# Fetching all channel weights at once on SyncE's queue, and converting them behind the attention's last cast

## The chip, the cores and the metric

The kernel runs on one core of one Trainium2 chip. The time is the device time of one execution in microseconds, lower is better. A core has five engines with a queue each: TensorE (PE in the profile; PEld is its weight load), VectorE (DVE), ScalarE (ACT), GpSimd (POOL) and SyncE (SP), which here only issues DMAs. Each engine runs its own queue in order; the engines meet through semaphores.

## What is computed

Three layers follow one another on four batches of 576 tokens with 512 channels: windowed attention, a layer of four attention experts of which each token uses two, and a mixing layer. The change lies at the passage from the second to the third, whose weights arrive in float64:

```python
# third layer
theta = x @ w_theta
zr, zi = x * cos(theta), x * sin(theta)
y = einsum('ts,bsd->btd', w_tok_r, zr) + einsum('ts,bsd->btd', w_tok_i, zi)
u = x + y
return u + maximum(u @ w_ch, 0)          # w_ch: the channel weights, 512 x 512
```

## The kernel before

All products run in a split form: an operand is a high part (rounded to the matmul's format) and a low part (the rest), and `mm3` (L97) adds three products, high by high (L98), high by low (L99) and low by high (L100). `split` (L90) makes the two parts, the high one mostly by an ACT cast (L92), the low one by a subtraction on DVE or POOL (L95).

The order of each engine's queue is fixed when the kernel is built: a planner goes through the traced operations by priority (the order in the program, where `merge` interleaves several generators by their costs) and puts each operation down when its operands and its place in memory are free by the planner's own clock. `tc.issue_after(x)` adds the rule that what is traced inside stands behind x on x's engine. At run time each engine follows its fixed order and waits where data are late.

The stages around the change, in order of time. `attn(3, 1)` is the last of the experts' attention, five steps t = 0 to 4, each ending with the cast of its output `oh` (L92, by way of L492). Beside it run `load_tok` (the token weights `w64k`, nine loads of 576 KB, converted in `load64`), `fuse` (products of `w_o` and `w_theta`, which read `wtl` for the last time), then `wo(3)` (output products, stored to DRAM from `xs3a` and `xs3b`) and `theta(0, 0)`. In `theta(b, dh)` five angles come one after the other: products into a bank `bs`, the ACT activation L640, the DVE subtraction L641 (which frees the bank), the ACT sine and absolute value L643 to L645, the DVE product L648 with a transposed `xk` (L636, bank `tb`), an ACT cast and a POOL subtraction into `z`. The fifth angle's products are the small `zf` (L662). Two places hold `ang`, for two angles each. Then `mix(0, 0)` multiplies `z` with the token weights, beside `theta(0, 1)`, `mix(0, 1)` follows beside `theta(1, 0)`, and `channel(0)` multiplies with the channel weights. `halves` makes further token weights in `x2a`, `x2b` and `wtl`.

`load_ch` (L835) brings the channel weights in eight half rows of 128 x 256 float64 (256 KB each) and hands each to `load64` (L105): one DMA from ACT's queue (L108; `late`, set in the attention, makes it stand behind an early exponential), two ACT multiplications (L122, L123), a DVE shift (L124) and a DVE merge of the sign (L130), a POOL addition (L132), an ACT cast (L137) and a DVE subtraction (L138). The staging places are two: for even k one place `bmsx` that holds the raw data and the working data, for odd k the places `VD0` (raw) and `VD1` (working). A load can thus be issued only when the conversion two before it has ended. Three conversions are traced beside `mix(0, 0)`, five beside `mix(0, 1)`.

Of the kernel before, what the change touches and what calls it, by code (L numbers as in the profile page):

```python
# [3 lines left out]

# [9 lines left out]
U32 = mybir.dt.uint32  # L14
I32 = mybir.dt.int32
U64 = mybir.dt.uint64
# [5 lines left out]
P = 128  # L22
# [11 lines left out]
NC = DM // P  # L34
# [6 lines left out]
def f32(ap):  # L41
    return ap.bitcast(F32)


def merge(*parts):

    live = [[0.0, float(total), gen] for total, gen in parts]
    while live:
        p = min(live, key=lambda x: x[0] / x[1])
        cost = next(p[2], None)  # L50
        if cost is None:
            live.remove(p)
        else:
            p[0] += cost
# [3 lines left out]
def kernel(ctx, tc, qT, kT, vw, consts, w_in, w_o, w_th, w_tk, w_ch, outT):  # L58
    nc = tc.nc

    cp = ctx.enter_context(tc.tile_pool(name="cp", bufs=1, side="left"))
# [16 lines left out]
    wtl = cp.tile([P, NC, DM], F32R, tag="wtl", name="wtl")  # L78
# [7 lines left out]
    def pool_mul(out, in_, by):  # L86
        nc.gpsimd.tensor_scalar(out=out, in0=in_, scalar1=by, scalar2=1.0,  # L87
                                op0=ALU.mult, op1=ALU.mult)

    def split(dst_h, dst_l, src, eng_h, eng_l):  # L90
        if eng_h is nc.scalar:
            nc.scalar.copy(out=dst_h, in_=src)  # L92
        else:
            eng_h.tensor_copy(out=dst_h, in_=src)
        return eng_l.tensor_sub(out=dst_l, in0=src, in1=f32(dst_h))  # L95
# [7 lines left out]


    def load64(kind, st, tu, dst_h, dst_l, src, scale=1.0):  # L105
        if late[0]:
            with tc.issue_after(late[0].ins):
                nc.scalar.dma_start(st, src)  # L108
        else:
            with tc.issue_after(last_load[0].ins):  # L110
                nc.sync.dma_start(st, src)
        v = st.bitcast(U32).rearrange("p (n two) -> p n two", two=2)
        lo, hi = v[:, :, 0], v[:, :, 1]
        n = KN["DP"][kind]
        step = st.shape[1] // n
        full = lo, hi, tu[:, 0], tu[:, 1], dst_h, dst_l
        for k in range(n):
            lo, hi, t, u, dst_h, dst_l = (x[:, step * k : step * k + step] for x in full)
            if KN["DM"][kind]:
                nc.gpsimd.tensor_scalar(out=f32(t), in0=f32(hi), scalar1=2.0**-112, scalar2=1.0, op0=ALU.mult, op1=ALU.mult)  # L120
            else:
                nc.scalar.mul(out=f32(t), in_=f32(hi), mul=2.0**-112)  # L122
            nc.scalar.mul(out=u, in_=lo, mul=2.0**-29)  # L123
            shift = lambda: nc.vector.tensor_scalar(out=t, in0=t, scalar1=3, scalar2=None, op0=ALU.logical_shift_left)  # L124
            if kind == 1 and gated[0]:
                with tc.issue_after(gated[0].ins):
                    shift()
            else:
                shift()
            nc.vector.scalar_tensor_tensor(out=t, in0=hi, scalar=0x80000000, in1=t,  # L130
                                           op0=ALU.bitwise_and, op1=ALU.bitwise_or)
            nc.gpsimd.tensor_add(out=t.bitcast(I32), in0=t.bitcast(I32), in1=u.bitcast(I32))  # L132
            if scale == 1.0:
                if KN["DH"][kind]:
                    nc.vector.tensor_copy(out=dst_h, in_=f32(t))
                else:
                    nc.scalar.copy(out=dst_h, in_=f32(t))  # L137
                (nc.vector if KN["DL"][kind] else nc.gpsimd).tensor_sub(out=dst_l, in0=f32(t), in1=f32(dst_h))  # L138
            else:
                nc.scalar.activation(out=dst_h, in_=f32(t), func=AF.Copy, scale=scale)  # L140
                nc.vector.scalar_tensor_tensor(out=dst_l, in0=f32(t), scalar=scale, in1=f32(dst_h),
                                               op0=ALU.mult, op1=ALU.subtract)
# [20 lines left out]
    bp = tc.alloc_tile_pool(name="bp", bufs=1, side="right")  # L163
# [54 lines left out]
    last_v = [None]  # L218
    late = [None]
    gated = [None]  # L220
    X = {b: xbuf[b % 2] for b in range(B)}

    ahead = {}
# [188 lines left out]
    def attn(b, ep):  # L412
# [7 lines left out]
        for t in range(5):  # L420
# [11 lines left out]
            for i in range(2):  # L432
                e = 2 * ep + i
                n = f"{b}{e}{t}"
# [55 lines left out]
                          pT[:, j, i, :m], start=(j == t - 1), stop=False)  # L490
            nc.tensor.matmul(o[:, :m], VD[ep][:, t].rearrange("p h d -> p (h d)"), pT[:, t, 0, :m], start=(t == 0), stop=True)
            split(oh[:, q0 : q0 + m], ol[:, q0 : q0 + m], o[:, :m], nc.scalar, nc.vector)  # L492
            if t == 4:
                for k, x in enumerate((oh, ol)):
                    nc.sync.dma_start(od[b][:, 2 * ep + k], f32(x))
            yield 0.4 * (t + 1)

    def wo(b):
        for n0, n1 in ((0, 320), (320, 576)):
            for m in range(NC):  # L500
                g = bank([P, n1 - n0], ("gggg", ("as", "ta", "g", "g"), ("as", "g", "ta", "g"))[KN["WB"][b]][m], f"x2{b}{m}{n0}")
                for c in range(2):
                    oh, ol = O[b, c]
                    mm3(g, woh[c][:, m * P : (m + 1) * P], wol[c][:, m * P : (m + 1) * P],
                        oh[:, n0:n1], ol[:, n0:n1], c == 0, c == 1)
                nc.scalar.copy(out=x2T[b][:, m, n0:n1] if b < 2 else xs[b][m // 2][:, m % 2, n0:n1], in_=g)
                if b > 1 and n1 == S and m % 2:
                    nc.sync.dma_start(xd[b][:, m - 1 : m + 1], xs[b][m // 2])
                yield 0.75


    HW = DM // 2
# [44 lines left out]
    def load_pair(b):  # L557
        xt = kp.tile([P, NC, P], F32, tag="xt", name=f"xt{b}")
        xo = kp.tile([P, 4, P], F32R, tag="xo", name=f"xo{b}")
        for k in range(2):  # L560
            sl = slice(64 * k, 64 * k + 64)
            if b == 0:
                pool_mul(xt[:, :, sl], x2T[b + k][:, :, W4:], 1.0)
            else:
                nc.sync.dma_start(xt[:, :, sl], xd[b + k][:, :, W4:])
            nc.sync.dma_start(f32(xo[:, :, sl]), od[b + k][:, :, W4:])
        XT[0] = xt, xo
# [262 lines left out]
    def load_tok(cs):  # L830
        for c in cs:
            load64(1, *staging(f"k{c}", S), wkh[c], wkl[c], w_tk[c * P : (c + 1) * P])
            yield 1.0

    def load_ch():  # L835
        for k in range(2 * NC):
            c, sl = k // 2, slice(HW * (k % 2), HW * (k % 2) + HW)
            if k % 2:
                st = bp.tile([P, HW], U64, tag="VD0", name=f"w64c{k}")
                tu = bp.tile([P, 2, HW], U32, tag="VD1", name=f"wtuc{k}")  # L840
            else:
                su = rp.tile([P, 2, HW], U64, tag="bmsx", name=f"w64c{k}")
                st, tu = su[:, 0], su[:, 1].bitcast(U32).rearrange("p (two n) -> p two n", two=2)
            load64(2, st, tu, wch[c][:, sl], wcl[c][:, sl], w_ch[c * P : (c + 1) * P, sl])
            yield 0.5

    def delay(cost, gen):
# [65 lines left out]
                  "x2a": (rp, 1), "x2b": (rp, 1), "x3a": (kp, 1), "x3b": (kp, 1)})  # L913
    load_o(3)
    load_pair(0)
    merge((KN["WO"][3], wo(3)), (KN["CW"][0], theta(0, 0)))
    wc = [bp.tile([P, DM], F32R, tag=f"wo{x}{c}", name=f"wc{x}{c}") for c in range(2) for x in "hl"]
    wd = [bp.tile([P, 2, DM], F32R, tag="vg", bufs=2, name=f"wd{c}") for c in range(2)]
# [79 lines left out]
```

## Time and profile before

| | us |
|---|---|
| median of 3 runs | 512.54 |
| lowest and highest run | 511.04, 513.37 |
| the profiled execution | 512.65 |
| its span in the trace | 510.9 |

In the profile a line such as L108 is a line of the kernel's file. Views in order of time give start, duration, engine, line, operation, output and input by the program's names, and in brackets the idle time of the engine just before with what ended it. ACTq and SPq are the queues' own work, such as issuing a DMA. Raw channel data are `w64c` (working data of even k too, since both share a place), the working data of odd k are `wtuc`; `wch` and `wd` are high parts, `wcl` and `wd` low parts. The granted TensorE clock is 1.00 in all stretches read below.

### The profile page before, as it was taken

The page shows a single profiled execution, that of the slowest core. Times are in us where ns is not written, and L with a number is a line of the kernel's source. Part 1 is how long each engine was busy: PE and PEld are TensorE (multiplying, and loading weights), DVE is VectorE, ACT ScalarE, POOL GpSimd, SP SyncE. Part 2 cuts the span into 40 slices and gives each one's busy share as a digit, 9 for nine tenths or more (in the row PEclk, how much of TensorE's full clock was granted, in tenths as well). Part 3 has the DMA queues.
Part 4 walks back from the last instruction along what each step waited for, and adds up shares of the span by engine and source line. Part 5 has one row for each costly group of instructions (what it writes and reads, how often), then busy time and mean ns, then how long its engine had stood idle before and what let it go on. Part 6 is the DMA issues. An engine that isn't in the chain of part 4 may idle for free.

```text
span 510.9 us, 12108 instructions
## 1 busy us (share of the span) xinstructions
PE 482.4 (94%) x4128; PEld 446.9 (87%) x4128; DVE 368.0 (72%) x1274; ACT 346.9 (68%) x1072; POOL 328.1 (64%) x455
## 2 busy tenths in 40 slices
PE   7898899999999999999999999799999989999997
PEld 5687888889898999988878779699999889899997
DVE  4766887866977768745888775878569948884832
ACT  6947787866787868857786796786276716762720
POOL 6758799864685863335683556578649926792770
PEclk9999999999999999999999999999999999999999
DMA  7665233431335341111245735431353044202002
GB/s 249 191 199 164 82 122 112 128 112 63 121 90 185 111 162 53 33 48 48 68 137 182 262 108 188 135 86 42 97 172 80 6 140 129 63 23 94 1 0 94
DMA packets 45470, 55.92 MB, mean 109 GB/s; under 512 B 6496, under 2 KB 34144, under 8 KB 45408
## 3 DMA queue, kind: packets, MB, share of 16 engines
q1 hardware_dynamic: 43392, 50.36, 31.8%
q10 hardware_dynamic: 2016, 4.79, 2.8%
q8 instruction: 33, 0.54, 0.5%
q14 instruction: 29, 0.24, 0.2%
HBM read 43.34 MB, written 11.80 MB: 108 GB/s over the span
## 4 chain that ended last, share of the span: by engine, by line
PE 50%; DVE 20%; ACT 12%; POOL 7%; DMA 5%; issue 5%; SPq 0%; POOLq 0%; DVEq 0%; ACTq 0%
PE as L272 3%; PE bpt L473 3%; PE qk L98 2%; ACT ams L285 2%; PE apt L297 2%; PE qk L99 2%; PE qk L100 2%; PE bs L441 2%; DMA wst<-in_dram 2%; PE c L98 2%; DMA w64c<-in_dram 2%; PE ao L153 2%; PE c L100 2%; DVE ang L648 2%; PE c L99 2%
## 5 line engine op out<-in xcount | busy, mean ns | idle before, releaser
L285 ACT ACTIVATE ams<-ams,anm 128x128 f32<-128x128 f32 x144 | 56.6, 396 | 6.1 <-DVE anm L277 4.8
L292 POOL TENSOR_TENSOR ams<-ams,arc 128x384 f32<-128x384 f32 x48 | 40.4, 844 | 25.5 <-DVE arc L291 11.5
L87 POOL TENSOR_SCALAR QD<-qt 64x192 f32<-64x192 f32 x72 | 39.7, 551 | 19.2 <-PE as L272 12.5
L450 ACT ACTIVATE bms<-bms,bnm 64x64 f32<-64x64 f32 (+4 forms) x80 | 44.8, 561 | 9.2 <-DVE bnm L445 8.7
L272 PE MATMUL as<-kt,QD 128*128 128x128 f32 x288 | 42.1, 283 | 4.0 <-ACT x0h L92 1.3
L277 DVE CUSTOM_DVE_ANT_0 ams<-as,cst 128x128 f32<-128x128 f32 x144 | 34.9, 284 | 11.8 <-PE apt L297 8.0
L272 PEld LDWEIGHTS as<-kt,QD 128*128 128x128 f32 x288 | 37.0, 194 | 7.3 <-ACT x0h L92 1.5
L445 DVE CUSTOM_DVE_ANT_0 bms<-bs,mb 64x64 f32<-64x64 f32 (+4 forms) x80 | 32.6, 423 | 7.6 <-PE bs L443 4.5
L462 POOL TENSOR_SCALAR bpd<-bms,bsm,gw 128x64 f32<-128x64 f32 (+1 forms) x47 | 21.8, 465 | 23.0 <-DVE bsm L455 10.6
L95 POOL TENSOR_TENSOR cu<-x2T,cu 128x288 fp32r<-128x288 f32 x32 | 29.5, 934 | 9.3 <-ACT cu L92 9.3
L441 PE MATMUL bs<-KA,QS 128*128 128x288 f32 (+4 forms) x96 | 31.8, 340 | 0.4 <-DVE bnm L445 0.2
L98 PE MATMUL y<-wkh,z 128*128 128x288 f32 x108 | 32.1, 300 | 0.0
L100 PE MATMUL y<-wkh,z 128*128 128x288 f32 x108 | 31.9, 300 | 0.0
L99 PE MATMUL y<-wkl,z 128*128 128x288 f32 x108 | 31.9, 296 | 0.0
L760 POOL TENSOR_TENSOR x2T<-x2T,u 128x288 f32<-128x288 f32 x20 | 16.6, 840 | 21.8 <-DVE u L771 19.3
L473 PE MATMUL bpt<-cst,bms 128*128 128x128 f32 x160 | 27.8, 278 | 2.8 <-POOL bms L462 1.2
L640 ACT ACTIVATE ang<-th,magic 128x256 f32<-128x256 f32 x36 | 16.6, 467 | 20.4 <-PE th L100 18.9
L443 PE MATMUL bs<-KL,QS 128*128 128x288 f32 (+4 forms) x96 | 27.6, 295 | 0.1
L285 ACT ACTIVATION_READ_ACCUMULATOR ams<-ams,anm 128x1 f32 x144 | 27.5, 191 | 0.0
L812 DVE SCALAR_TENSOR_TENSOR x2T<-c,x2T 128x288 f32<-128x288 f32 x32 | 13.9, 453 | 17.2 <-PE c L100 17.0
L648 DVE TENSOR_TENSOR ang<-xk,ang 128x512 f32<-128x512 f32 x32 | 21.7, 684 | 5.9 <-ACT ang L645 5.8
L462 POOL TENSOR_SCALAR bms<-bms,bsm,gw 128x384 f32<-128x384 f32 (+3 forms) x40 | 25.7, 642 | 0.0
(339 smaller groups left out, 2034.4 us busy)
## 6 DMA issues: line engine op xcount, KB each, us to landing
vt<-in_dram SPq DMA_DIRECT2D x48, 192.0 KB, 3.1
or<-od SPq DMA_DIRECT2D x32, 256.0 KB, 3.4
kt<-in_dram SPq DMA_DIRECT2D x15, 320.0 KB, 3.2
qt<-in_dram SPq DMA_DIRECT2D x16, 288.0 KB, 3.3
out_dram<-x2T SPq DMA_DIRECT2D x32, 144.0 KB, 1.7
w64k<-in_dram SPq DMA_DIRECT2D x5, 576.0 KB, 3.7
od<-oh SPq DMA_DIRECT2D x8, 288.0 KB, 2.9
od<-ol SPq DMA_DIRECT2D x8, 288.0 KB, 3.9
```

The source lines that it names most:

```text
L87: nc.gpsimd.tensor_scalar(out=out, in0=in_, scalar1=by, scalar2=1.0, op0=ALU.mult, op1=ALU.mult)
L98: nc.tensor.matmul(out, wh, xh, start=first, stop=False)
L99: nc.tensor.matmul(out, wh, xl, start=False, stop=False)
L100: nc.tensor.matmul(out, wl, xh, start=False, stop=last)
L272: nc.tensor.matmul(s[:, i, :], QD[g][:, i], kt[:, 64 * blk : 64 * blk + 128], start=True, stop=True)
L277: nc.vector.tensor_tensor_reduce(out=ms[:, i, :], in0=s[:, i, :], in1=ma0 if (g == 0 and i == 0) else ma1, scale=-0.125, scalar=3.0e38, op ...
L285: nc.scalar.activation(out=ms[:, i, :], in_=ms[:, i, :], func=AF.Exp, bias=nm[:, i : i + 1], scale=-1.0, accum_out=sm[:, i, 0:1],)
L292: nc.gpsimd.tensor_mul(out=ms, in0=ms, in1=rc.unsqueeze(2).to_broadcast([P, 3, P]))
L441: nc.tensor.matmul(s[:m, : z - a], qs[:, q0 : q0 + m], ka[:, a:z], start=True, stop=False)
L450: ex = nc.scalar.activation(out=ms[:m, :w], in_=ms[:m, :w], func=AF.Exp, bias=nm[:m, ci : ci + 1], scale=-1.0, accum_out=ss[:m, i, 0:1])
L462: eng.tensor_scalar(out=dst, in0=src, scalar1=sm[:m, i : i + 1], scalar2=gw[:m, t, 2 * ep + i : 2 * ep + i + 1], op0=ALU.mult, op1=ALU.mult)
L473: nc.tensor.transpose(pt[:, jj, i, :], pn[:, i, P * j : P * j + P], ident)
```

## The change

All eight raw half rows are fetched in a new function `fetch_ch`, called before `wo(3)` and `theta(0, 0)` are traced. They get a place each: two in `x2a` and two in `x2b` (their tenants have been stored to DRAM), four in `wtl`. The DMAs are issued on SP's queue. `load64` gets no source any more for these and issues nothing. The working place is `bmsx` for even k and `VD1` for odd k. The two ACT multiplications of each conversion stand behind `closed`, the last attention cast traced.

```diff
+    cast = [None]
+
     def split(dst_h, dst_l, src, eng_h, eng_l):
         if eng_h is nc.scalar:
-            nc.scalar.copy(out=dst_h, in_=src)
+            cast[0] = nc.scalar.copy(out=dst_h, in_=src)
...
     def load64(kind, st, tu, dst_h, dst_l, src, scale=1.0):
-        if late[0]:
+        if src is None:
+            pass
+        elif late[0]:
...
-                nc.scalar.mul(out=f32(t), in_=f32(hi), mul=2.0**-112)
-            nc.scalar.mul(out=u, in_=lo, mul=2.0**-29)
+                with tc.issue_after(closed[0].ins) if kind == 2 else nullcontext():
+                    nc.scalar.mul(out=f32(t), in_=f32(hi), mul=2.0**-112)
+            with tc.issue_after(closed[0].ins) if kind == 2 else nullcontext():
+                nc.scalar.mul(out=u, in_=lo, mul=2.0**-29)
...
             split(oh[:, q0 : q0 + m], ol[:, q0 : q0 + m], o[:, :m], nc.scalar, nc.vector)
+            closed[0] = cast[0]
...
+    def fetch_ch():
+        for t in "ab":
+            a = rp.tile([P, 2, HW], U64, tag=f"x2{t}", name=f"w64c{t}")
+            raw.extend(a[:, k] for k in range(2))
+        a = cp.tile([P, 4, HW], U64, tag="wtl", name="w64c")
+        raw.extend(a[:, k] for k in range(4))
+        for k in range(2 * NC):
+            c, sl = k // 2, slice(HW * (k % 2), HW * (k % 2) + HW)
+            nc.sync.dma_start(raw[k], w_ch[c * P : (c + 1) * P, sl])
+
     def load_ch():
         for k in range(2 * NC):
             c, sl = k // 2, slice(HW * (k % 2), HW * (k % 2) + HW)
-            if k % 2:
-                st = bp.tile([P, HW], U64, tag="VD0", name=f"w64c{k}")
-                tu = bp.tile([P, 2, HW], U32, tag="VD1", name=f"wtuc{k}")
-            else:
-                su = rp.tile([P, 2, HW], U64, tag="bmsx", name=f"w64c{k}")
-                st, tu = su[:, 0], su[:, 1].bitcast(U32).rearrange("p (two n) -> p two n", two=2)
-            load64(2, st, tu, wch[c][:, sl], wcl[c][:, sl], w_ch[c * P : (c + 1) * P, sl])
+            st = raw[k]
+            tu = (rp, bp)[k % 2].tile([P, 2, HW], U32, tag=("bmsx", "VD1")[k % 2], name=f"wtuc{k}")
+            load64(2, st, tu, wch[c][:, sl], wcl[c][:, sl], None)
             yield 0.5
...
     load_pair(0)
+    fetch_ch()
     merge((KN["WO"][3], wo(3)), (KN["CW"][0], theta(0, 0)))
```

## Rows read from the trace of the kernel before

**Rows 1.** Busy time of TensorE, share of the span, instructions (the page, part 1).
```profile
PE 482.4 (94%) x4128; PEld 446.9 (87%) x4128; DVE 368.0 (72%) x1274; ACT 346.9 (68%) x1072; POOL 328.1 (64%) x455
```

**Rows 2.** Busy time by stretch (instructions), granted clock, DMA share, GB/s.
```profile
300.00:305.00 5.00, 5.00 (x49) 4.59 (x47) 1.74 (x3) 5.00 (x16) 2.17 (x2) 1.00 0.37 107
...
310.00:315.00 5.00, 5.00 (x40) 5.00 (x39) 1.48 (x3) 1.76 (x4) 4.27 (x4) 1.00 0.97 338
...
sum 40.00, PE 35.79 PEld 34.18 DVE 26.53 ACT 30.38 POOL 23.81; mean PE 4.47 PEld 4.27 DVE 3.32 ACT 3.80 POOL 2.98
```

**Rows 3.** Chain of waits, 262 to 345 us: start, duration, what.
```profile
309.90 6.72 DMA w64c<-in_dram
...
322.85 2.65 DMA w64c<-in_dram
```

**Rows 4.** ACT in order of time, 295 to 345 us.
```profile
306.15 0.28 ACT L92 CAST oh<-o 128x128 fp32r<-128x128 f32 x1
...
309.47 0.82 ACTq L108 DMA_DIRECT2D w64c<-in_dram  x2
...
314.69 0.43 ACT L122 ACTIVATE wtuc<-w64c 128x256 f32<-128x256 f32 x1 [2.87 <-DMA w64c<-in_dram]
315.03 0.46 ACT L640 ACTIVATE ang<-th,magic 128x256 f32<-128x256 f32 x1
316.65 0.43 ACT L122 ACTIVATE w64c<-w64c 128x256 f32<-128x256 f32 x1 [1.16 <-DMA w64c<-in_dram]
...
329.12 0.45 ACT L640 ACTIVATE ang<-th,magic 128x256 f32<-128x256 f32 x1
```

**Rows 5.** PE in order of time, its stalls in 300 to 345 us.
```profile
306.59 0.44 PE L636 MATMUL xk<-cst,x2T 128*128 128x128 f32 x2 [0.43 <-DVE ang L648]
...
316.30 0.39 PE L98 MATMUL th<-wot,or 128*128 128x256 f32 x1 [0.32 <-DVE ang L641]
...
321.25 0.41 PE L636 MATMUL xk<-cst,x2T 128*128 128x128 f32 x2 [1.60 <-DVE zf L662]
...
330.93 0.39 PE L98 MATMUL th<-wot,xo 128*128 128x256 f32 x1 [1.86 <-DVE ang L641]
```

**Rows 6.** DVE and POOL in order of time, 296 to 345 us.
```profile
305.19 0.66 DVE L124 TENSOR_SCALAR w64c<-w64c 128x256 uint32<-128x256 uint32 x1 [1.73 <-ACT w64c L122]
...
319.36 1.75 DVE L662 TENSOR_TENSOR zf<-xk,ang 64x256 f32<-64x256 f32 x4
...
330.46 0.41 DVE L641 SCALAR_TENSOR_TENSOR ang<-ang,th 128x256 f32<-128x256 f32 x1
...
310.29 3.98 POOL L95 TENSOR_TENSOR z<-ang,z 128x512 fp32r<-128x512 f32 x3
```

**Rows 7.** Instructions on w64c: count, ns min/median/max, first and last start.
```profile
L108 ACTq DMA_DIRECT2D w64c<-in_dram x8: 334/334/389, 281.9 to 329.9; - x8
...
L132 POOL TENSOR_TENSOR w64c<-w64c x4: 732/738/747, 307.0 to 335.2; 128x256 int32<-128x256 int32 x4
```

**Rows 8.** SP's queue in order of time, and PE's last product on wtl.
```profile
274.24 0.33 SPq L508 DMA_DIRECT2D xd<-xs2b  x1
...
290.74 6.29 SPq L553 DMA_DIRECT2D or<-od  x4
...
284.41 0.39 PE L99 MATMUL wot<-wtl,woT 128*128 128x512 f32 x1
```

**Rows 9.** Busy time by stretch, 282 to 290 us.
```profile
282.00:284.00 2.00, 2.00 (x12) 1.66 (x11) 0.52 (x2) 1.29 (x4) 0.00 (x0) 1.00 1.09 408
...
288.00:290.00 2.00, 2.00 (x15) 1.70 (x14) 2.00 (x5) 1.91 (x6) 1.10 (x1) 1.00 0.25 104
```

**Rows 10.** ACT in order of time, 276 to 296 us.
```profile
283.38 0.72 ACT L122 ACTIVATE wtuk<-w64k 128x576 f32<-128x576 f32 x1 [0.54 <-DMA w64k<-in_dram]
...
290.88 0.73 ACT L122 ACTIVATE wtuk<-w64k 128x576 f32<-128x576 f32 x1 [0.97 <-POOL wkl L138]
```

**Rows 11.** Busy time by stretch, a later stage.
```profile
400.00:410.00 10.00, 8.40 (x62) 7.94 (x60) 9.82 (x18) 5.73 (x13) 9.27 (x10) 1.00 0.01 2
```

More of the change, by code (lines that the diff above doesn't have):

```diff
@@ L1 @@
 import math
-from contextlib import ExitStack
+from contextlib import ExitStack, nullcontext
 from itertools import islice
@@ L220 @@
     gated = [None]
+    closed = [None]
     X = {b: xbuf[b % 2] for b in range(B)}
@@ L833, in load_tok @@
             yield 1.0
+    raw = []
+    def fetch_ch():
[7 more added lines that the diff above has]
+            nc.sync.dma_start(raw[k], w_ch[c * P : (c + 1) * P, sl])
     def load_ch():
```

## The prediction

> **What bounds the kernel now.** I read four views in this order: the page's busy shares, the busy times stretch by stretch, the chain of waits, and the rows of each engine in order of time.
>
> TensorE is busy for 94% of the span [rows 1], so the first question is where the other 6% lies. The change touches the loading and conversion of the channel weights, which the trace shows from the first load at 281.9 to the last addition at 335.2 us [rows 7]. In 300 to 340 us TensorE is busy for 35.79 of 40.00 us, so 4.21 us are idle; in 310 to 315 us ScalarE (ACT) is busy for only 1.76 and VectorE (DVE) for 1.48 of 5 us, while the 16 DMA engines have a share of 0.97 [rows 2]. Something waits there for data. The chain of waits names it: a channel-weight load of 6.72 us that ends in ACT's multiplication at 316.65, and another of 2.65 us that ends at 325.52 [rows 3].
>
> ACT's own rows show how this comes about. Two loads are issued together at 309.47, only then because two of the staging places had been held by the first two conversions. ACT then reaches the multiplications that need them and stands idle 2.87 us until 314.69 and 1.16 us until 316.65 [rows 4]. ACT runs its queue in order, so what is behind these instructions waits too: the fifth magic-number activation of theta(0, 0) (L640) runs at 315.03 although nothing else holds it. Its place in `ang` is free when GpSimd (POOL) ends the first of the three splits that begin at 310.29 and take 3.98 us in all, at about 310.29 + 3.98 / 3 = 311.6 [rows 6]; ACT itself is free at 314.69 - 2.87 = 311.8. So theta's chain is held for about 315.03 - 311.8 = 3.2 us.
>
> What reaches the end is what TensorE loses. Its four stalls in this stretch are 0.43, 0.32, 1.60 and 1.86 us [rows 5], together 4.21 us, the whole idle time of rows 2. The first follows a DVE product that ran behind a weight shift of 0.66 us at 305.19. The second and third follow the late L640: DVE's L641 frees the bank for the next theta, and the four `zf` products, late at 319.36, free the next `xk`. The fourth follows an L641 at 330.46 [rows 6]. It had its ACT input at about 329.12 + 0.45 = 329.57 [rows 4], but DVE had conversion work in front.
>
> **The change, part by part.** *The fetch.* Eight DMA issues leave ACT's queue, 0.334 us each, 2.7 us of issuing in all [rows 7], and go to SP's. ACT's issues overlap its running instructions in the rows, so I count nothing for them. On SP they stand behind the stores that read the earlier tenants of `x2a` and `x2b` (the last issued at 274.24), and four of them wait until the last product that reads `wtl`, at 284.41 [rows 8]. SP's next work is ring loads from 290.74 on [rows 8]; they would have to be issued after the fetches, which are gone from the queue by about 284.8 + 4 x 0.33 = 286. An attention store stands near them too, but its readers come much later. So SP's queue costs nothing.
>
> *The load waits.* All 2 MB are in place some 15 us before the first multiplication. The 2.87 and 1.16 us of ACT go, as does the 2.65 us in the chain. What is late next: for theta's fifth angle it is POOL's split at 311.6, 3.2 us earlier than now. Second and third stall, 0.32 + 1.60 us, are shorter than these 3.2 us, so I take both as gone. The fourth has two bounds: at least the 330.46 - 329.57, about 0.85, that DVE spent on conversions; at most its 1.86 us, if L640 too comes earlier, since ACT runs conversion work immediately ahead of it. I take the middle, 1.35.
>
> *The hold.* The 16 multiplications of the conversions must now stand behind the last attention cast, which runs at 306.15 [rows 4]. It is an order on ACT's own queue, where nobody stands waiting at run time. The rows of before show one pair of multiplications and the DVE shift of 305.19 ahead of that cast; they move behind it, and with the shift goes the first stall, 0.43 us. ACT is full in 300 to 305 us (5.00 of 5 [rows 2]), so two multiplications less, 0.34 us apart by 314.69 and 315.03 in rows 4, can help by up to 0.7 us there; I count that only in a rival. Behind the moved pair stand ACT's casts of `z` and then POOL's splits; ACT has the 4.0 us of the removed waits to give back, and that hides it. If that cover were gone, one conversion would cost three such steps, about 1 us of ACT.
>
> *Conversion places.* Only two result places remain, so two conversions are under way at once, as before. Each needs a 0.74 us addition on POOL [rows 7]: 5.9 us for eight, the same as before. The last addition now starts at 335.2 [rows 7] and none of the stalls of rows 5 is at a product with these weights, so the end of the conversions has slack.
>
> *The collision.* The early 2 MB meet the token-weight loads. In 282 to 284 us the DMA share is 1.09 at 408 GB/s, in 288 to 290 us only 0.25 [rows 9]. At 283.38 ACT is already waiting 0.54 us for a token load, and at 290.88 it waits 0.97 us for POOL, so the next load there had slack [rows 10]. The lower bound is 0, if the fetches go into the slack. The upper is 0.52 MB / 0.4 = 1.3 us on the first pair of token loads and 1.05 MB / 0.4 = 2.6 us on the third, 3.9 us on an ACT queue that holds the attention's exponentials. Nearest is rows 9: by 286 us there are 0.52 MB more and 0.26 MB less (the load issued at 281.9 is gone), 0.26 / 0.408 = 0.64 us, of which I charge half, 0.3, as ACT waited there anyway and TensorE had the weight product to run.
>
> The Trainium skill, page "DMA: Bandwidth & Descriptors", section "Issuing engines are not separate DMA queues", says that DMAs started from different engines run on the same 16 engines and interleave, and that spreading them saves only issue time. That speaks against this change: SP's queue brings no bandwidth of its own. The 1.09 share in a stretch with stores from SP and loads from ACT fits it. By that rule the upper bound of the collision counts, the fourth case below.
>
> *Sum.* 0.43 + 0.32 + 1.60 + 1.35 = 3.7 us gained, 0.3 lost: 3.4 us. Against the profiled execution, 512.65 us, that is 509.25; its time stands 0.11 above the median of the runs, so I say 509.2. For this to reach the end, the later stretches must take an earlier start: TensorE is the full engine in most of what follows, but in 400 to 410 us DVE is busy for 9.82 of 10 and TensorE for 8.40 [rows 11]. All of DVE's work there is fed by the same chain and shifts with it, so I take no loss there, only width.
>
> **The rivals.** *The full gain.* All 4.21 us of idle time go, and the attention tail ends up to 0.7 us sooner: 512.65 - 4.2 to - 5.6 (0.7 on each of ACT and the chain behind), 507.0 to 508.4. For it speaks that ACT is full there; against it that some stall usually forms behind a filled one.
>
> *The hole is filled by the conversions themselves.* With all data present, the fixed order may put conversions 3 to 5 on ACT ahead of the fifth L640. Each takes about 1 us of ACT, so three take back the 3.2 us. Only the first stall would go: 512.2, between 511 and 513.5. For it speaks that POOL is busy with splits until 314.3 and that the conversions are free to run; against it that theta stands earlier in the program for part of them.
>
> *The token weights come late; slower.* The fetches of 278 to 288 us push the token loads, ACT stands at their multiplications at 283.38 and 290.88, and behind it in order stand the cast of the fused weights and the exponentials. Price 1.3 + 2.6 = 3.9 us. With the forecast's gains kept this gives 512.65 - 3.7 + 3.9 = 512.9; with none of them 516.5, since a theta that starts 3.9 us later brings the stalls of rows 5 back. I take 515.2, nearer to the second for this reason. It turns slower when these two waits grow by more than 3.7 us together, or by less if the stalls come back. Against it: the first pair is already under way when the larger half is fetched, and the DMA engines are idle soon after.
>
> *The change does not do what it says*: the fetches are issued late. Nothing on SP's queue or in the three places gives a reason, so I give it no chance of its own.
>
> **How the numbers follow.** What a measurement of this kernel can tell from no change is about 0.5%, 2.56 us: under 509.98 is faster, over 515.10 slower. Forecast: 0.48, with its own range of 508.2 to 510.7, 0.40 of it under 509.98. Full gain: 0.12. Filled hole: 0.22. Late token weights: 0.18, 0.13 of it over 515.10. So faster 0.40 + 0.12 = 0.52, same 0.08 + 0.22 + 0.05 = 0.35, slower 0.13. The range goes from 506.9, which takes in the full gain, to 515.0; about 0.14 is left out above and 0.03 below.
>
> **What would show it.** Right: no ACT row with a wait for `w64c`; the fifth L640 within 1 us of POOL's second `z` split; the stalls at L636 and at theta's products in the 40 us after the attention's end under 1.5 us in all; all eight channel loads on SP before 290 us. Wrong: conversions ahead of the fifth L640 with TensorE idle behind (filled hole); ACT waits for `w64k` over 1 us near 283 and 291 us (late token weights); or stalls shortened here and a longer DVE wait in 380 to 450 us, which would be a gain given back.

## The result, and the profile after

| | before | after |
|---|---|---|
| median, us (7 runs each) | 512.97 | 508.69 |
| lowest and highest run, us | 511.04, 513.37 | 506.32, 509.97 |
| the profiled execution, us | 512.65 | 506.32 |
| its span in the trace, us | 510.9 | 504.5 |

The ratio of the times is 0.9916 with a 95% interval of 0.9891 to 0.994: 4.3 us faster by the medians, where 3.4 us were forecast. The profiled execution of the changed kernel is the fastest of its seven, 2.4 us under their median, so its span shows more gain than the medians do. Where that comes from is told with the stages, below.

In the changed kernel's file most lines are shifted: L643 to L645 became L651 to L653, L636 is L644, L640 is L648, L641 is L649, L648 is L656, L662 is L670, L686 is L694; `mm3`'s products are L100 to L102, a conversion's instructions L127, L129 (multiplications), L130, L136, L138, L143 and L144, the fetch L853.

Busy time of TensorE, the page of the kernel after, as [rows 1]:

```profile
PE 480.7 (95%) x4128; PEld 446.4 (88%) x4128; DVE 373.6 (74%) x1274; ACT 346.4 (69%) x1072; POOL 328.4 (65%) x455
```

Busy time by stretch of the kernel after (PE, PEld, DVE, ACT, POOL with instructions, granted clock, DMA share, GB/s); the sum is over 300 to 340 us, as [rows 2], the last row answers to [rows 11]:

```profile
310.00:315.00 5.00, 5.00 (x40) 5.00 (x39) 4.97 (x6) 3.08 (x9) 4.07 (x4) 1.00 0.16 62
...
sum 40.00, PE 37.78 PEld 36.48 DVE 33.73 ACT 33.63 POOL 27.37; mean PE 4.72 PEld 4.56 DVE 4.22 ACT 4.20 POOL 3.42
...
400.00:410.00 10.00, 8.71 (x66) 8.50 (x66) 6.75 (x14) 2.24 (x5) 5.92 (x6) 1.00 0.20 72
```

TensorE's idle time in 300 to 340 us has gone from 4.21 us [rows 2] to 40.00 - 37.78 = 2.22 us, a gain of 1.99 and not of 3.7. In 310 to 315 us, where ACT and DVE had been idle for most of the time, DVE is now busy for 4.97 of 5 us. The stalls that are left, TensorE of the kernel after in order of time, as [rows 5], and one later one:

```profile
304.75 0.74 PE L100 MATMUL x<-oh,woh 128*128 128x256 f32 x4 [0.17 <-ACT oh L94]
...
308.98 0.44 PE L644 MATMUL xk<-cst,xt 128*128 128x128 f32 x2 [1.05 <-DVE ang L656]
...
326.61 0.39 PE L100 MATMUL th<-wot,xo 128*128 128x256 f32 x1 [0.70 <-DVE ang L649]
...
404.86 0.37 PE L100 MATMUL c<-cu,wch 128*128 128x288 f32 x1 [1.29 <-DVE zf L670]
```

Up to 340 us there is one more stall, of 0.17 us at 327.76. The two stalls that followed the late L640 (0.32 and 1.60 us in [rows 5]) have gone, the fourth fell from 1.86 to 0.70. The first did not go: it moved to a later product and grew from 0.43 to 1.05. ACT of the kernel after in order of time, as [rows 4, 10]:

```profile
281.62 0.72 ACT L127 ACTIVATE wtuk<-w64k 128x576 f32<-128x576 f32 x1 [0.52 <-DMA w64k<-in_dram]
...
283.85 0.76 ACT L127 ACTIVATE wtuk<-w64k 128x576 f32<-128x576 f32 x1 [0.90 <-DMA w64k<-in_dram]
...
289.79 0.74 ACT L127 ACTIVATE wtuk<-w64k 128x576 f32<-128x576 f32 x1 [0.80 <-DMA w64k<-in_dram]
...
304.40 0.30 ACT L94 CAST oh<-o 128x128 fp32r<-128x128 f32 x1
304.54 0.49 ACT L127 ACTIVATE wtuc<-w64ca 128x256 f32<-128x256 f32 x1
...
305.20 0.48 ACT L127 ACTIVATE wtuc<-w64ca 128x256 f32<-128x256 f32 x1
...
310.77 0.43 ACT L127 ACTIVATE wtuc<-w64cb 128x256 f32<-128x256 f32 x1 [0.24 <-DVE wcl L144]
...
311.44 0.45 ACT L648 ACTIVATE ang<-th,magic 128x256 f32<-128x256 f32 x1
```

No multiplication waits for a channel weight any more. The fifth magic-number activation (L648) runs at 311.44. The cast of the last attention output (L94, `oh`) has the multiplications of two conversions directly behind it, and DVE and then POOL of the kernel after in order of time show what that does, as [rows 6]:

```profile
306.36 0.53 DVE L130 TENSOR_SCALAR wtuc<-wtuc 128x256 uint32<-128x256 uint32 x1
306.92 1.41 DVE L136 SCALAR_TENSOR_TENSOR wtuc<-w64ca,wtuc 128x256 uint32<-128x256 uint32 x1
308.24 1.28 DVE L656 TENSOR_TENSOR ang<-xk,ang 128x512 f32<-128x512 f32 x2
...
324.83 1.39 DVE L136 SCALAR_TENSOR_TENSOR wtuc<-w64c,wtuc 128x256 uint32<-128x256 uint32 x1
326.14 0.41 DVE L649 SCALAR_TENSOR_TENSOR ang<-ang,th 128x256 f32<-128x256 f32 x1
```

```profile
306.69 1.35 POOL L97 TENSOR_TENSOR z<-ang,z 128x512 fp32r<-128x512 f32 x1
...
309.15 4.18 POOL L97 TENSOR_TENSOR z<-ang,z 128x512 fp32r<-128x512 f32 x3
...
323.30 2.64 POOL L97 TENSOR_TENSOR z<-ang,z 128x512 fp32r<-128x512 f32 x2 [1.04 <-ACT z L94]
```

The shift and the sign merge of the second conversion (k = 1), the merge with 1.41 us, run immediately ahead of the angle product L656, and TensorE's `xk` at 308.98 waits for this L656. The fourth stall has the same form: a merge of 1.39 us stands ahead of the L649 for which TensorE waits at 326.61. Both merges run beside a POOL split (306.69 and 323.30). Over the traces of all kernels, each of the 60 sign merges of channel weights with no POOL instruction beside it took 0.41 to 0.43 us, and the 18 longest, of 1.38 to 1.42 us, all had POOL busy beside them for over 1 us. A merge of 0.43 us would have let this L656 start 1.41 - 0.43 = 0.98 us earlier, nearly the whole stall of 1.05 us (an estimate). SP's queue of the kernel after issues the eight loads in 272.6 to 286.8 us, as [rows 8]:

```profile
272.55 0.33 SPq L853 DMA_DIRECT2D w64ca<-in_dram  x1
...
279.25 0.80 SPq L853 DMA_DIRECT2D w64cb<-in_dram  x2
...
283.19 3.63 SPq L853 DMA_DIRECT2D w64c<-in_dram  x4
```

**The stages.** The two kernels execute the same 4128 matmuls, so the start of a matmul of the same number can be compared; up to each of the numbers used here the sets of matmuls agree but for one at most. The table gives by how much each stretch of the profiled execution became longer (+) or shorter (-) than in the kernel before, in us. The stretches end at matmuls 2400, 2700, 2850, 3300 and the last; their times in the kernel before stand above. The last columns are the sum without the first stretch, and the difference of the medians (each kernel against the runs of the kernel before beside it). The experiments' rows are used further down.

| kernel | 0-267 | -309.5 | -333 | -394 | -end | sum without first | by medians |
|---|---|---|---|---|---|---|---|
| after | -1.62 | -0.42 | -1.87 | +0.06 | -2.48 | -4.7 | -4.3 |
| r_after (the same kernel) | -0.73 | +1.31 | -1.85 | +0.07 | -2.56 | -3.0 | -3.2 |
| r_after_b (the same kernel) | -0.50 | -0.56 | -1.72 | +0.05 | -2.52 | -4.8 | -4.9 |
| e_nohold | +0.43 | -0.85 | -3.95 | 0.00 | -1.88 | -6.7 | -5.9 |
| e_holdonly | -1.51 | -0.99 | -1.29 | +1.66 | -2.51 | -3.1 | -3.5 |
| e_latefetch | +0.02 | -1.09 | -3.36 | +1.46 | -0.11 | -3.1 | -2.7 |
| e_split | -1.48 | -0.23 | -1.69 | +0.06 | -2.50 | -4.4 | -4.5 |
| e_split_nohold | -1.56 | -0.92 | -3.95 | +0.02 | -1.85 | -6.7 | -6.1 |
| e_fifth | -1.41 | -0.29 | +0.55 | +1.36 | -2.49 | -0.9 | -1.2 |
| e_actq | +0.22 | -0.45 | -1.78 | +0.06 | -1.06 | -3.2 | -3.0 |
| e_behind | -1.52 | -1.03 | -1.68 | +0.02 | -2.48 | -5.2 | -4.6 |
| e_behind_nohold | -0.60 | -0.66 | -3.96 | +0.04 | -1.88 | -6.5 | -6.3 |

In the first stretch the queues hold the same instructions in the same order in all of them, so its up to 2 us are differences between executions. Without it, the sums agree with the medians within 0.8 us. So the forecast's place, up to 333 us, gave about 2.3 us (0.42 + 1.87), and a stretch that the forecast had put at nothing, the last, gave 2.5.

### The profile page after: what moved, and what is told of

Read it like the earlier page. It is cut to its first block, busy times and chain, and to the rows that moved or that the text cites. A ratio compares the mean times of both kernels' runs of the same rounds, so it can differ in the third digit from the quotient of the medians.

```text
span 504.5 us, 12104 instructions
## 1 busy us (share of the span) xinstructions
PE 480.7 (95%) x4128; PEld 446.4 (88%) x4128; DVE 373.6 (74%) x1274; ACT 346.4 (69%) x1072; POOL 328.4 (65%) x455
## 4 chain that ended last, share of the span: by engine, by line
PE 51%; DVE 20%; ACT 11%; POOL 9%; issue 5%; DMA 4%; SPq 0%; POOLq 0%; DVEq 0%; ACTq 0%
PE as L279 4%; PE bpt L480 3%; PE qk L100 2%; PE c L100 2%; DMA w64k<-in_dram 2%; PE qk L101 2%; PE apt L304 2%; PE c L102 2%; PE qk L102 2%; PE c L101 2%; ACT ams L292 2%; PE ao L159 2%; DMA wst<-in_dram 2%; PE bs L448 2%; DVE ang L656 2%
## 5 line engine op out<-in xcount | busy, mean ns | idle before, releaser
L100 PE MATMUL y<-wkh,z 128*128 128x288 f32 x108 | 32.1, 302 | 0.2 <-DVE x2T L694 0.2
L102 PE MATMUL y<-wkh,z 128*128 128x288 f32 x108 | 31.3, 297 | 0.0
L648 ACT ACTIVATE ang<-th,magic 128x256 f32<-128x256 f32 x36 | 16.7, 466 | 17.9 <-PE th L102 17.5
L656 DVE TENSOR_TENSOR ang<-xk,ang 128x512 f32<-128x512 f32 x32 | 21.7, 684 | 8.2 <-ACT ang L653 6.2
```

Source lines behind the costliest of these rows:

```text
L100: nc.tensor.matmul(out, wh, xh, start=first, stop=False)
L102: nc.tensor.matmul(out, wl, xh, start=False, stop=last)
```

## The experiments

Three questions were put: which of the two parts, early fetch or hold, pays and how (first four runs); whether the gain is the load wait itself, and whether the loads disturb the token weights (the next four); and what the best of these are worth side by side (the last three). "Fetch" is the change with its places and SP's queue, "hold" the two `issue_after(closed)`.

### The parts, one by one

**The changed kernel again** (`r_after`). No edit; it stands beside the others of this set on the same chip.

> The changed kernel unaltered, for a second profile and a tighter ratio. Queue orders of both kernels are the same up to about 264 us, yet the two profiles differ by 1.6 us there. Theory A (that 1.6 us is a difference between executions, what follows is the change): ratio 0.990 to 0.993 (about 508.5 us), the start of the channel products again 3.5 to 4.5 us before the old one after the first 264 us are put level within 0.5 us, TensorE idle 2.0 to 2.6 us in 300 to 340 us. Rival (the stages after 380 us gained by chance of that execution): the 2.1 us that the first profile gained behind 390 us shrink under 1 us.

Measured: 508.54 us, ratio 0.9935 (0.9915 to 0.9955). As expected, TensorE's idle time in 300 to 340 us is 2.29 us, and the last stretch's gain came again (-2.56), so the rival fell; the ratio lies just above its range of 0.990 to 0.993. The profiled execution holds something that the first did not, here ACT in order of time:

```profile
283.25 0.72 ACT L127 ACTIVATE wtuk<-w64k 128x576 f32<-128x576 f32 x1 [1.28 <-DMA w64k<-in_dram]
...
286.18 0.72 ACT L127 ACTIVATE wtuk<-w64k 128x576 f32<-128x576 f32 x1 [1.59 <-DMA w64k<-in_dram]
...
292.39 0.75 ACT L127 ACTIVATE wtuk<-w64k 128x576 f32<-128x576 f32 x1 [1.11 <-DMA w64k<-in_dram]
```

ACT waits 4.0 us for token weights, where the first profile of this kernel has 2.2 us and the kernel before 0.54 in the first of these places [rows 10]. TensorE in order of time and the busy times by stretch of this run show that it reaches the end:

```profile
288.04 0.77 PE L100 MATMUL th<-wot,or 128*128 128x256 f32 x2 [1.65 <-ACT wot L94]
```

```profile
286.00:288.00 2.00, 0.38 (x2) 0.15 (x2) 1.21 (x6) 1.82 (x4) 0.82 (x1) 1.00 1.09 397
288.00:290.00 2.00, 1.96 (x9) 1.96 (x10) 1.98 (x5) 2.00 (x5) 0.00 (x0) 0.53 0.97 323
290.00:292.00 2.00, 2.00 (x12) 2.00 (x12) 0.80 (x4) 1.28 (x5) 1.75 (x2) 0.62 0.91 304
```

The cast of `wot` stands behind the waiting multiplications, TensorE is idle 1.65 us, and then its granted clock is 0.53 and 0.62 for 4 us, the matmuls there being at the lower of its two levels for the most part. In this execution the two loads into `x2b` were issued at 278.52, just ahead of the first token load at 278.59; in the first profile the two token loads (277.72 and 278.27) went ahead of them (279.25). These are the waits of the rival of the late token weights. The second stretch is 1.7 us longer than in the first profile (+1.31 against -0.42); how much of this is the stall and how much the lower clock behind it was not separated.

**Fetch without hold** (`e_nohold`).

```diff
-                with tc.issue_after(closed[0].ins) if kind == 2 else nullcontext():
+                with nullcontext():
                     nc.scalar.mul(out=f32(t), in_=f32(hi), mul=2.0**-112)
-            with tc.issue_after(closed[0].ins) if kind == 2 else nullcontext():
+            with nullcontext():
                 nc.scalar.mul(out=u, in_=lo, mul=2.0**-29)
```

> The early fetch alone, without the order of the multiplications behind the last attention cast. Theory A (the load waits on ACT are what cost): most of the gain stays, 508.5 to 510 us, no ACT wait for w64c, up to 0.7 us later in the attention's tail because conversions run on a full ACT before 304 us. Rival H (the hold keeps the attention's tail free and is what pays): 511 to 513 us, the last attention cast more than 1.5 us later than in the changed kernel.

Measured: 505.87 us, ratio 0.9889 (0.9872 to 0.9906), faster than the changed kernel and than both expectations. The sum of the busy times in 300 to 340 us, and DVE and then POOL in order of time:

```profile
sum 40.00, PE 39.88 PEld 38.65 DVE 33.23 ACT 35.14 POOL 28.13; mean PE 4.98 PEld 4.83 DVE 4.15 ACT 4.39 POOL 3.52
```

```profile
305.98 0.69 DVE L656 TENSOR_TENSOR ang<-xk,ang 128x512 f32<-128x512 f32 x1 [1.23 <-PE xk L644]
...
307.23 0.43 DVE L136 SCALAR_TENSOR_TENSOR wtuc<-w64ca,wtuc 128x256 uint32<-128x256 uint32 x1
307.57 0.68 DVE L656 TENSOR_TENSOR ang<-xk,ang 128x512 f32<-128x512 f32 x1
...
308.76 1.28 DVE L656 TENSOR_TENSOR ang<-xk,ang 128x512 f32<-128x512 f32 x2
```

```profile
307.83 0.73 POOL L138 TENSOR_TENSOR wtuc<-wtuc 128x256 int32<-128x256 int32 x1 [0.78 <-PE x L102]
```

TensorE is idle for 0.12 us of 40 and no stall is left. The first conversion's multiplications run at 303.5 and 303.8, ahead of the last cast at 305.92. With its shift and merge out of the way, those of the second conversion run one angle product earlier, ahead of the L656 at 307.57, while POOL is idle (0.78 us up to 307.83), and the merge takes 0.43 us instead of 1.41. The L656 at 308.76, for which `xk` waits in the changed kernel, no longer stands behind them. The hold binds only the first conversion, since all others stand behind the last cast here as well. So the hold, which moves two multiplications, a shift and a merge a few places back, costs 2.1 us in 309.5 to 333 us (-1.87 against -3.95), with the order of the queues that the planner makes around it. It gives back 0.6 us in the last stretch.

**Hold without fetch** (`e_holdonly`): the kernel before, with `closed` and the two `issue_after` of the change's diff, and nothing else of it.

> The kernel before with the hold alone: two staging places and loads from ACT's queue stay, the multiplications stand behind the last attention cast. Theory A: the ACT waits for w64c of 2 to 4 us stay or grow, 512 to 514 us. Rival H: 508.5 to 510.5 us.

Measured: 508.31 us, ratio 0.9937 (0.992 to 0.9955), as fast as the changed kernel beside it. ACT in order of time:

```profile
310.88 0.47 ACT L646 ACTIVATE ang<-th,magic 128x256 f32<-128x256 f32 x1 [0.67 <-DVE wcl L142]
...
313.44 0.43 ACT L125 ACTIVATE wtuc<-w64c 128x256 f32<-128x256 f32 x1 [2.08 <-DMA w64c<-in_dram]
```

The load waits are still there (2.6 us in all), but the fifth magic-number activation (L646 here) now has its place ahead of them. Up to 333 us this kernel gains 2.3 us with the waits in place, but it gives 1.66 back by 394 us. Most of its gain, 2.51 us, is in the last stretch, which none of the theories had: the total lies near Rival H's range, but not for its reason.

**Late fetch** (`e_latefetch`). Places and hold as in the change, but the loads stand on SP behind the store of the last attention output, so that they are issued at 306.8 to 309 us.

```diff
-                    nc.sync.dma_start(od[b][:, 2 * ep + k], f32(x))
+                    stored[0] = nc.sync.dma_start(od[b][:, 2 * ep + k], f32(x))
...
-            nc.sync.dma_start(raw[k], w_ch[c * P : (c + 1) * P, sl])
+            with tc.issue_after(stored[0].ins):
+                nc.sync.dma_start(raw[k], w_ch[c * P : (c + 1) * P, sl])
```

> The changed kernel, but all eight loads are put on SP's queue behind the store of the last attention output (about 305 us) instead of 272 to 287 us: same eight places, same hold, late data. Theory A: the data come 5 to 8 us after the hold ends, waits on ACT come back, 511 to 514 us, and the token loads no longer wait (ACT waits for w64k under 0.6 us each). Rival (the empty places alone, so many loads in flight at once, are enough): 508 to 509.5 us.

Measured: 509.04 us, ratio 0.9946 (0.9932 to 0.996). The planner put the multiplications to 309.9 us and later, so nothing waits for the late loads, the premise of Theory A did not come about, and up to 333 us this kernel gains 4.5 us. It has the hold too, so the price of the hold hangs on where the instructions land. It gives 1.5 back by 394 us, and in the last stretch it gains nothing (-0.11). From about 355 us on its queues of TensorE, ACT, DVE and POOL have the order of the kernel before, and the waits of TensorE in 380 to 450 us (total, times, longest) are the same row by row, first before, then with the late fetch:

```profile
PE c L98 <- DVE zf L662: 1.4, 1, 1.4
PE xk L636 <- DVE zf L662: 1.2, 1, 1.2
...
PE yi L98 <- DVE x2T L754: 0.5, 1, 0.5
```

```profile
PE c L100 <- DVE zf L671: 1.4, 1, 1.4
PE xk L645 <- DVE zf L671: 1.2, 1, 1.2
...
PE yi L100 <- DVE x2T L763: 0.5, 1, 0.5
```

In the changed kernel the wait of `xk` for `zf` has shrunk to 0.4 us and that of `yi` is gone:

```profile
PE xk L644 <- DVE zf L670: 0.4, 1, 0.4
```

So the last stretch's 2.5 us belong in the main to the order in which the queues were laid out anew, not to an earlier start: the late fetch starts that stretch early too and has none of them.

### The wait, the queue and the collision

**Only L640 ahead of the wait** (`e_fifth`). The kernel before, with the multiplications of the conversions from the third on (k = 2 to 7) behind the fifth L640 of theta(0, 0).

```diff
-            nc.scalar.activation(out=rn, in_=th, func=AF.Identity, bias=magic)
+            act = nc.scalar.activation(out=rn, in_=th, func=AF.Identity, bias=magic)
+            if (b, dh, i) == (0, 0, 4):
+                fifth[0] = act
...
+            with tc.issue_after(fifth[0].ins) if kind == 2 and held[0] else nullcontext():
...
+            held[0] = k > 1
             load64(2, st, tu, wch[c][:, sl], wcl[c][:, sl], w_ch[c * P : (c + 1) * P, sl])
```

> The kernel before, its two staging places and loads unchanged; only conversions 2 to 7 have their ACT multiplications behind the fifth magic activation of theta(0, 0), so the load waits stay but theta's fifth angle is ahead of them. Theory B (a load wait costs by what is queued behind it, here that activation): the ACT waits for w64c stay 2 to 4 us, the TensorE stalls of 0.32 and 1.60 us go, 1.5 to 3 us gained by 340 us; in total 508.5 to 511.5 us, as the later order is planned anew too. Rival (the wait itself is what costs): 511.3 to 513 us and the stalls stay.

Measured: 510.69 us, ratio 0.9973 (0.9951 to 0.9994). ACT and then TensorE in order of time:

```profile
310.03 0.47 ACT L644 ACTIVATE ang<-th,magic 128x256 f32<-128x256 f32 x1
...
315.57 0.43 ACT L123 ACTIVATE w64c<-w64c 128x256 f32<-128x256 f32 x1 [5.07 <-DMA w64c<-in_dram]
```

```profile
320.88 0.41 PE L640 MATMUL xk<-cst,x2T 128*128 128x128 f32 x2 [3.37 <-DVE zf L668]
```

L640 (L644 here) ran 5.0 us earlier than in [rows 4], of which 1.7 us (1.41 + 0.29) come from the stretches before, and ACT then stood 5.07 us at the load, with the sine and absolute value of the same angle behind it in the queue. TensorE's stall for `zf` grew from 1.60 to 3.37 us. So the price of such a wait is set by everything that stands behind it, and the forecast's wording, that L640 was held, was too narrow. Up to 394 us this kernel loses (+0.55 and +1.36), and yet it gains 2.49 in the last stretch, where all four engines have the very order of the changed kernel: the second sign that this gain is one of order. The total lies in Theory B's range by luck, since the stall for `zf` that was to go has grown, and TensorE's idle time in 300 to 340 us is 4.99 us, where it was 4.21.

**Loads on ACT's queue** (`e_actq`). The changed kernel, with the eight loads issued by ACT behind `late`.

```diff
-            nc.sync.dma_start(raw[k], w_ch[c * P : (c + 1) * P, sl])
+            with tc.issue_after(late[0].ins):
+                nc.scalar.dma_start(raw[k], w_ch[c * P : (c + 1) * P, sl])
```

> The changed kernel with the eight loads on ACT's queue instead of SP's, as soon as their places are free; places and hold unchanged. If the queue matters (Theory Q: an issue on ACT that waits for its place holds the attention's exponentials behind it, the last four places are free only at 284 us): 510 to 513 us with ACT idle 1 to 4 us more in 272 to 290 us. If it does not (the same DMA engines serve both queues): 508 to 509.5 us.

Measured: 508.89 us, ratio 0.9936 (0.9913 to 0.9958), beside 0.9916, 0.9935 and 0.9894 of the changed kernel: no difference that can be told, and no more idle time of ACT in 272 to 290 us than in the changed kernel (12.38 us busy against 11.91), so Theory Q falls. The Trainium skill, page "DMA: Bandwidth & Descriptors", section "Issuing engines are not separate DMA queues", says that starting DMAs on several engines at once saves only the time of issuing them. The ratios agree with it, but the pair differs in more than the queue: the loads were issued at 280.6 to 289.3 us, and the planner laid out the other queues anew from about 286 us on.

This run also shows that order isn't all of the last stretch's gain. From about 367 us on its four engines have the order of the kernel without hold, and yet it gains 1.06 us there and not 1.88. The difference is one wait of TensorE, which is 0.4 us there, and here (waits in 380 to 505 us):

```profile
PE xk L644 <- DVE zf L670: 1.2, 1, 1.2
```

On DVE's queue ahead of it some instructions took longer and others less long, one of them more than three times as long, first without hold, with POOL idle, then here, with POOL splits beside it:

```profile
423.15 0.41 DVE L610 TENSOR_TENSOR ang<-ang 128x256 f32<-128x256 f32 x1
```

```profile
424.46 1.51 DVE L610 TENSOR_TENSOR ang<-ang 128x256 f32<-128x256 f32 x1
```

That this is what lengthens the wait was not tested.

**Most loads later, with and without hold** (`e_split`, `e_split_nohold`). Six of the eight loads stand on SP behind the ring load that is issued near 289 us; two stay where they were.

```diff
+            ring_load[0] = nc.sync.dma_start(f32(o), od[b][:, :, i * P : i * P + P])
...
+                if (b, dh, i) == (0, 0, 1):
+                    load_raw(range(2, 2 * NC), ring_load[0])
...
+            with tc.issue_after(behind.ins) if behind else nullcontext():
+                nc.sync.dma_start(raw[k], w_ch[c * P : (c + 1) * P, sl])
```

> The changed kernel with one difference, in SP's queue alone (all other queue orders are the same): six of the eight loads go behind the first ring load that waits (about 289 us) instead of 279 to 287 us, so they no longer meet the first three token loads. Theory C (the early loads collide with the token loads, 0.7 to 1.8 us in the two profiles): 506.5 to 508 us, ACT waits for w64k under 0.6 us in all as before, the stalls after 300 us unchanged, less spread between executions. Rival O (the collision is hidden, the whole distance between the changed kernel and the one without the hold is the order after 300 us): 508.5 us. Rival D (all of that distance is the collision): 505.5 to 506.2 us.

> The kernel without the hold with the same six loads moved in SP's queue alone. Theory C: 504.5 to 505.8 us, a little under the kernel without the hold (505.9), since its profile showed little of the collision (0.4 us of waits). Rival (late data, the third conversion waits): over 506.5 us with ACT waits for w64c.

Measured: 507.4 us, ratio 0.9902 (0.9881 to 0.9924), and without the hold 505.83, 0.9879 (0.9854 to 0.9903). ACT's waits for token weights are 1.1 and 0.5 us. The first time lies in Theory C's range, but its interval overlaps those of the changed kernel; the second is that of the kernel without hold (505.87), so moving the loads gained nothing there that can be told. The hold costs the same here as before: -1.69 against -3.95 in 309.5 to 333 us.

### The best ones side by side

The same as the split, with all eight loads behind that ring load (289.5 to 294 us), with and without hold (`e_behind`, `e_behind_nohold`), and the changed kernel a third time (`r_after_b`).

> The changed kernel once more, beside the two below on the same chip, since the loads' position was worth about as much as the uncertainty. Theory C (early loads collide with token loads): ratio 0.991 to 0.9935, ACT waits for w64k of 1.5 to 4 us in 276 to 294 us, 508 to 509 us.

> The changed kernel with all eight loads behind the first waiting ring load in SP's queue (about 289 us); all other queue orders are the same. Theory C: no more meeting with the first three token loads, ACT waits for w64k under 0.8 us, the stretch up to 289 us as in the kernel before within 0.4 us, 506.5 to 507.8 us, at least 0.8 us under the changed kernel of the same call. Rival O: 508 to 509 us, as the changed kernel.

> The same without the hold: TensorE idle under 0.4 us in 300 to 340 us as in the other kernels without it, 504.5 to 506 us, 1.5 to 2.5 us under the kernel with all loads behind and the hold (Theory: the hold's place for the first conversion costs about 2.1 us between 309 and 333 us). Rival (the difference was chance): within 1 us of it.

Measured: 507.1 us, 0.9894 (0.9872 to 0.9917) for the changed kernel; 507.34, 0.9894 (0.987 to 0.9918) with the loads behind; 505.66, 0.9869 (0.9843 to 0.9895) with the loads behind and no hold. ACT's waits for token weights fall from 2.0 us to 0.3 between the first two, and their medians agree, where Theory C had at least 0.8 us between them: the collision is in single profiles, but its average price isn't measurable. The changed kernel itself came out under what was expected for it (508 to 509 us). The last is the best kernel of the study, 1.3% under the kernel before; the two others without hold are the same within their intervals.

## Why the prediction was right, and where it was not

The total came out near the forecast (508.69 against 509.2, within its own range of 508.2 to 510.7), but not by its sum: the stage came out 1.6 us short of it and a later stage that was put at nothing gave 2.5 us. That the two offset each other to within 1 us is luck. (509.25 less the 0.11 is 509.14 and not 509.2, and the lower bound of the fourth stall is 0.89 and not 0.85; neither matters.) Point by point:

- *What bounds the kernel.* Right: ACT's queue stood at two loads, and it cost TensorE time. Over the runs, ACT's waits for channel weights and TensorE's idle time in 300 to 340 us go together in the kernels without the hold behind the last cast: 5.4 and 4.99 us in the run with L640 ahead, 4.0 and 4.21 before, none and 0.12 with the early fetch alone. Too narrow was that L640 alone was held.
- *The load waits*, 0.32 + 1.60 us. Right: both stalls are gone.
- *The fourth stall*, forecast at 1.35 of its 1.86 us. It gave 1.16; mechanism and size hold.
- *The hold*, the step that failed. It was to take the first stall with it (0.43 us gained), and its two displaced multiplications were to be hidden in ACT's freed time. ACT did hide them. What I left out is where the shifts and merges land on DVE's queue: those of the second conversion came ahead of the L656 that the next `xk` needs, and beside a POOL split, where the merge took 1.41 us. The stall is 1.05 us. The run without the hold shows it: the merge 0.43 us, no stall there, and 2.1 us in this stretch, in which the other stalls are gone too. That POOL stretches the merge is read from the traces and was not tested by itself. The new stalls are 2 x 0.17. The sum of the stage thus is -0.62 + 1.92 + 1.16 - 0.34 = 2.12, by the busy times 1.99, where 3.7 stood.
- *The collision*, 0.3 us. The mechanism is there: token-load waits of 2.2, 4.0 and 2.0 us in the three profiles of the changed kernel, though only 0.4 us in that of the kernel without hold, which has the same fetch. In the second one the waits near 283 and 292 us passed 1 us each, the sign named for the slower rival, and its stretch came out 1.7 us longer than in the first. On average it isn't to be told from nothing, so the term was sized as well as it can be. The price of 3.9 us was not reached.
- *The later stages*, "no loss, only width": wrong in the other direction, 2.5 us gained. DVE's full stretch of 400 to 410 us (9.82 of 10, TensorE 8.40, [rows 11]) became 6.75 and 8.71, but since the stretches are shifted by 4 to 5 us these are not the same work. The two stalls of 1.4 and 1.2 us for `zf` became 1.29 and 0.4. I compared the work of the stages, which is unchanged, and not their order, which the planner laid out anew for the four engines from about 305 us to the end. That the order and not an earlier start is the main cause rests on three runs: the late fetch has the old order and no gain there, the hold alone has an order of its own and 2.51 us, and the run with L640 ahead has the changed kernel's order and 2.49 us, although it comes to this stretch no earlier than the kernel before. The run with the loads on ACT's queue shows that some 0.8 us of such a gain can be lost under one and the same order. Which of the reordered instructions does it was not isolated and stays open.

So 3.4 us forecast were 3.7 - 0.3; in the first profile they were 2.3 up to 333 us (the collision within it) and 2.5 after. The rival of the full gain describes the kernel without the hold almost exactly in this stage (0.12 us of idle time left). The filled hole did not come about: TensorE is busy for 5.00 of 5 us in 310 to 315 us. The fifth L640 runs 0.9 us after the POOL split that frees its place (309.15 + 4.18 / 3 = 310.5), within the 1 us that was named. One sign of being right failed: the stalls at L636 and at theta's products were to be under 1.5 us in all, and are 1.05 + 0.70 = 1.75 us, for the reason given at the hold.

## What to carry to other kernels

Price a wait in an in-order queue by all that stands behind it, and an instruction that is moved by where its consumers on the other queues land, here a DVE shift and merge ahead of the product that TensorE needed next, and beside a POOL split that went with a merge three times as long. When a planner lays out the queues, even a small rule re-orders all that follows: compare the order of the later stages before their cost is put at nothing, and test each part of a change alone, since here the early fetch without the hold was the faster kernel.

## What was not expected of the hardware

- Executions of the same instructions in the same order differ by up to 2 us over the first 267 us (-1.62 to +0.43 in the table). Part of it goes with the clock: in the two highest (+0.43 and +0.22) the granted clock fell near 65 us, here the kernel without hold:

```profile
62.00:64.00 2.00, 0.42 (x3) 0.14 (x1) 1.87 (x11) 1.55 (x5) 2.00 (x5) 1.00 0.23 86
64.00:66.00 2.00, 2.00 (x11) 2.00 (x12) 1.90 (x9) 1.98 (x9) 1.84 (x5) 0.65 0.00 0
```

  In the kernel before TensorE was busy for 0.49 of 2 us in the same place, and its clock stayed at 1.00. The rest is not the clock: the profiles with -1.62, -0.50 and +0.02 and that of the kernel before all have 1.00 there. A single profile says little about a gain of this size until that stretch is taken off.
- In the second profile of the changed kernel, TensorE had been busy for 0.38 of 2 us, and its granted clock was then 0.53 (near the lower of its two levels, 1.2 of 2.4 GHz) and 0.62 for 4 us, back at 1.00 from 292 us. The longer stall of 3.37 us in the run with L640 ahead was not followed by this. Busy times by stretch of the latter:

```profile
318.00:320.00 2.00, 0.00 (x0) 0.00 (x0) 1.00 (x4) 1.56 (x5) 0.72 (x1) 1.00 0.32 114
...
322.00:324.00 2.00, 2.00 (x18) 2.00 (x17) 1.51 (x5) 1.92 (x6) 0.29 (x2) 1.00 0.40 131
```

- A DVE instruction of one and the same size took 0.41 to 0.43 us or up to 1.42 us, and the long ones had POOL at work beside them (the sign merges, above).
- Which of two queues issues first by a microsecond went along with the length of the waits in one and the same kernel: ACT waited 4.0 us for token weights where the loads into `x2b` were issued 0.07 us ahead of the first token load, and 2.2 and 2.0 us where they came 1.5 us (279.25 - 277.72) and 1.2 us behind it. In the kernel without hold they came 0.96 us behind it, and ACT waited 0.4 us. So this is a pattern of few profiles and not shown as the cause, and the distance alone does not set the wait.
